# Window attention, softplus layer and four experts on one core: all eighteen attention groups scheduled ahead of the dense layers, a third buffer for k and q chunks

## Chip, cores, metric

One core of one Trainium2 chip. The metric is the device time of one execution in microseconds (us). TensorE (PE) multiplies matrices, VectorE (DVE), ScalarE (ACT) and GpSimd (POOL) do element-wise work, SyncE (SP) issues the transfers. PEld is the loading of PE's weights, which overlaps PE.

## What is computed

```python
# attention, window 64, 2 batches, 8 heads, 576 positions, head size 64
scores = where(mask, q @ k.T / 8, -1e9); attn = softmax(scores); x = attn @ v    # x: 1152 x 512
h = x @ w_in                                                                      # 512 -> 2048
g = maximum(h, 0) + log1p(exp(-abs(h)))                                           # softplus
x1 = g @ w_out                                                                    # 2048 -> 512
p = domain_probs / (domain_probs.sum(-1) + 1e-9)
out = sum over 4 experts e of p[:, e] * (maximum(x1 @ w1[e], 0) @ w2[e])          # 512 -> 1024 -> 512
```

All inputs are float32, except that `w_in` and `w_out` come as 64-bit words, whose upper and lower halves the kernel turns into pairs of float32 itself.

## The kernel before

**Attention.** 18 groups of 64 positions each. A group has three pieces of PE work: scores `s` (L961, from a chunk of k, `kT`, and of q, `qT`, each serving three groups), transposes `p` (L989) and the product with v `o` (L1001). Between them DVE masks and takes the largest score (L968, four per group), ACT takes exponentials (L972, four), DVE inverts the sums (L976, L977), the four halves of `p` are scaled (L984 on ACT, L980 on DVE or POOL), the transposed `pT` is copied out of PSUM (L248), and the result `o` is split into a high part (L248 copy) and a low part (L1013, DVE) of `x`, in three blocks `x0`, `x1`, `x2` of 384 positions.

**The softplus layer**, the first dense stage. Its weights come in 16 chunks: two transfers into a raw buffer `r` (three of them), then `convert`: magnitude (L390, ACT), and on DVE hold (L394), rest (L397), place (L401), sign (L405), power (L408), whole (L411) and low (L414); the high part is copied by ACT or POOL. Then 4 units x 3 blocks x 4 chunks = 48 steps. A step is 12 matmuls `h` (L467), the softplus chain (ACT: L486, L489, L495, L501; DVE: lost L498, with_max L504; a subtraction `l<-l,w` and, after a cast by ACT to `g`, a subtraction `g<-l,g`, both at the helper's line L267), and 12 matmuls into four accumulators `acc` (L537). Sums over units go to `part` (L565).

**The experts**, the second dense stage, take seven products of halves instead of eight (L702, banks x, y, z) and 32 second products (L797); their weights are split into a high copy (L248) and a low subtraction (L267), with sums `S` of weight blocks.

**The order** of every engine's queue is made when the program is built. Each piece is an `Op` with the engines that may do it, and a due time; `plan` walks a model of the engines and always takes the piece that is ready and due first. Its numbers stand in `P`: `T0` is when the first dense step is due, `ATT` the spacing of attention groups before it, `E_...` which engines may do a kind of piece ("V" or "D" DVE, "A" ACT, "G" POOL). Groups 0 to 5 (block 0) are due before `T0`; groups 6 to 17 are due between the dense steps of unit 0. Each engine then runs its queue strictly in that order. A `Ring` says how many buffers a kind of tile has; a piece waits for the last reader of the buffer it takes.

Of the kernel before, what the change touches and what calls it, by code (L numbers as in the profile page):

```python
# [21 lines left out]
def kernel(  # L22
# [51 lines left out]
    AHEAD = 2  # L74
# [71 lines left out]
    class Ring:  # L146
# [10 lines left out]
        def take(self, first):  # L157
# [5 lines left out]
                                         we=EARLY, wl=LATE, p=3, pT=2, kT=2, v=5).items()}  # L163
# [191 lines left out]
    def convert(c, first, last, due):  # L355
# [97 lines left out]
    def step(s, u, blk, f, tag, due1, due2):  # L453
# [33 lines left out]

        def exponential():
# [22 lines left out]
        o1 = Op({"A": (ACT(tb, True), magnitude)}, [o] + re.next())  # L511
# [336 lines left out]
    def load_qk(c, due):  # L848
        b, s = c // CPB, (c % CPB) * CH

        def keys(k0, k1):
            if c not in kT:
                kT[c] = ap_.tile([128, NP, W + CH], F32, tag="kT", bufs=2, name=f"kT{c}")
            nc.sync.dma_start(out=kT[c][:, :, k0:k1], in_=k[b, :, :, s - W + k0:s - W + k1].rearrange("h p s -> p h s"))

# [13 lines left out]
        for k0, k1, g0, g1 in parts:  # L869
            there = [Op({"Q": ((k1 - k0) * 0.0057, lambda k0=k0, k1=k1: keys(k0, k1))}, after, due, 2.2)]  # L870
# [7 lines left out]
    def load_v(c, due):  # L878
        b = c // CPB
        for i in range((c % CPB) * GPC, (c % CPB + 1) * GPC):  # L880
# [11 lines left out]
            v_there[b, i] = Op({"Q": (0.75, fn)}, ring.next(), due, 2.2)  # L892
            v_done[b, i] = ring.take(v_there[b, i])

    class Group:
# [19 lines left out]
        def scores(self, due):  # L915
# [13 lines left out]
            for hp in range(NP):  # L929
# [3 lines left out]
                scaled.append(Op({e: how[e] for e in (P.E_P if self.blk else P.E_P0)}, [o]))  # L933
            self.p_there = scaled

        def transposes(self, due):
# [3 lines left out]
            o = Op(copies(512, self.transposed, True, P.E_T if self.blk else P.E_T0), [o] + pT.next())  # L940
# [3 lines left out]
        def values(self, due):  # L944
# [4 lines left out]
            o1 = Op(copies(KC * W, lambda: self.to_x()[1::-1], True, P.E_H if self.blk else P.E_H0), [o, *first_x[-1:]])  # L949
# [119 lines left out]
    groups = [Group(n, ("att", "h", "acc") if n < GPB[0] else ("att",) * 3) for n in range(NT // W)]  # L1069
    x_due0 = [P.T0 - P.ATT * (GPB[0] - 1 - n) for n in range(6)]  # L1070
# [120 lines left out]
```

## Time and profile before

| what | us |
|---|---|
| median of 3 runs (654.02 to 654.44) | 654.33 |
| the profiled execution, its time | 654.69 |
| its span in the profile | 652.6 |
| time around the span (difference) | 2.1 |
| PE busy / DVE busy / ACT busy / POOL busy | 629.6 / 505.3 / 356.9 / 192.6 |

The profile gives, for one execution, what each engine did and when. A row of instructions has a mean duration; neighbours on one engine overlap by their start-up, so the distance from one start to the next is some tenths of a microsecond shorter than the duration, and sums are made with that distance. Idle time of an engine is what is left of a window when its busy time is taken off.

### The profile page before, as it was taken

How to read it: one execution, taken by the hardware profiler on the slowest of the kernel's cores; microseconds unless marked ns; L12 is line 12 of the kernel's file. 1: busy time of each engine (PE TensorE's matmuls, PEld its weight loads, DVE VectorE, ACT ScalarE, POOL GpSimd, SP SyncE). 2: the span in 40 equal slices, each digit the busy share in tenths (PEclk: the TensorE clock that was granted, in tenths of full speed). 3: DMA queues.
4: the chain of work that ended last, by engine and by line, in shares of the span. 5: the costliest groups of instructions: out<-in, count | busy, mean ns of one | idle time of the engine just before them, and what ended most of it. 6: DMA issues, size and time to landing. Idle time of an engine off the chain costs nothing.

```text
span 652.6 us, 10673 instructions
## 1 busy us (share of the span) xinstructions
PE 629.6 (96%) x4008; PEld 577.7 (89%) x4008; DVE 505.3 (77%) x1002; ACT 356.9 (55%) x778; POOL 192.6 (30%) x166
## 2 busy tenths in 40 slices
PE   7679999999999999999999999999999999999997
PEld 6467889999999999898999989998989998989996
DVE  4999989999999998985756575585796687767643
ACT  6999988867676775643334244323634352535230
POOL 2212452101002641643305132160453342613310
PEclk9999999999999999999999999999999999999999
DMA  8954212222130410013112311231243313131001
GB/s 277 379 177 171 98 65 76 96 76 77 65 131 28 163 68 2 0 65 130 65 64 74 122 64 66 74 122 64 66 154 121 124 71 130 65 129 65 2 1 64
DMA packets 30515, 62.83 MB, mean 96 GB/s; under 512 B 2816, under 2 KB 6016, under 8 KB 30464
## 3 DMA queue, kind: packets, MB, share of 16 engines
q1 hardware_dynamic: 30464, 62.16, 27.0%
q8 instruction: 31, 0.51, 0.3%
q14 instruction: 20, 0.16, 0.1%
HBM read 59.79 MB, written 2.36 MB: 95 GB/s over the span
## 4 chain that ended last, share of the span: by engine, by line
PE 60%; DVE 28%; ACT 6%; issue 3%; DMA 2%; SPq 0%; DVEq 0%; ACTq 0%
PE acc L797 28%; PE y L702 11%; PE z L702 7%; PE x L702 7%; DVE w L498 3%; DVE g L267 3%; DVE l L504 3%; PE acc L537 2%; DVE part L565 2%; DVE kh L405 2%; DVE km L411 2%; DVE l L267 2%; DMA qT<-in_q_dram 2%; DVE w L414 2%; ACT p L972 2%
## 5 line engine op out<-in xcount | busy, mean ns | idle before, releaser
L797 PE MATMUL acc<-wb,G 128*128 128x512 f32 x864 | 213.6, 392 | 0.0
L797 PEld LDWEIGHTS acc<-wb,G 128*128 128x128 f32 x864 | 157.2, 188 | 28.7 <-DVE G L771 0.3
L537 PE MATMUL acc<-g,w 128*128 128x384 f32 x576 | 110.9, 340 | 2.2 <-DVE g L267 1.6
L467 PE MATMUL h<-x,w 128*128 128x384 f32 x576 | 105.9, 335 | 0.2 <-ACT w L248 0.2
L537 PEld LDWEIGHTS acc<-g,w 128*128 128x128 f32 x576 | 99.7, 188 | 5.9 <-DVE g L267 3.1
L267 POOL TENSOR_TENSOR wc<-S,wc 128x1024 fp32r<-128x1024 f32 x19 | 49.3, 2593 | 187.9 <-ACT wc L248 187.9
L467 PEld LDWEIGHTS h<-x,w 128*128 128x128 f32 x576 | 100.3, 188 | 0.9 <-ACT w L248 0.5
L767 ACT ACTIVATE G<-C 128x256 fp32r<-128x256 f32 (+2 forms) x64 | 35.8, 562 | 72.4 <-PE acc L797 50.2
L771 DVE SCALAR_TENSOR_TENSOR G<-C,G 128x256 fp32r<-128x256 f32 (+2 forms) x64 | 43.9, 686 | 30.2 <-ACT G L767 29.7
L248 ACT ACTIVATE wa<-rq 128x512 fp32r<-128x512 f32 x64 | 30.9, 515 | 59.9 <-PE y L702 56.1
L702 PE MATMUL y<-xo,wc 128*128 128x320 f32 (+1 forms) x384 | 62.1, 297 | 0.9 <-DVE q L723 0.8
L702 PE MATMUL z<-xo,wc 128*128 128x320 f32 (+1 forms) x384 | 61.6, 296 | 0.0
L267 POOL TENSOR_TENSOR l<-l,w 128x384 f32<-128x384 f32 x19 | 25.6, 1347 | 121.1 <-DVE l L504 100.7
L702 PE MATMUL x<-xo,wa 128*128 128x320 f32 (+1 forms) x384 | 61.3, 295 | 0.0
L702 PEld LDWEIGHTS x<-xo,wa 128*128 128x128 f32 x384 | 57.1, 189 | 3.4
L702 PEld LDWEIGHTS y<-xo,wc 128*128 128x128 f32 x384 | 55.4, 190 | 3.4 <-DVE q L723 1.6
L248 ACT ACTIVATE wc<-S 128x1024 fp32r<-128x1024 f32 x32 | 33.7, 1053 | 41.3 <-PE z L702 36.7
L702 PEld LDWEIGHTS z<-xo,wc 128*128 128x128 f32 x384 | 54.8, 190 | 0.1
L267 POOL TENSOR_TENSOR wa<-rq,wa 128x512 fp32r<-128x512 f32 (+1 forms) x32 | 38.8, 1220 | 26.4 <-ACT wa L248 22.8
L771 DVE SCALAR_TENSOR_TENSOR G<-x,G 128x320 fp32r<-128x320 f32 (+1 forms) x32 | 14.6, 457 | 34.2 <-ACT G L767 34.2
L767 ACT ACTIVATE G<-x 128x320 fp32r<-128x320 f32 (+1 forms) x32 | 13.1, 411 | 47.4 <-PE x L702 47.4
L267 DVE TENSOR_TENSOR wb<-rq,wb 128x1024 fp32r<-128x1024 f32 x29 | 35.4, 1222 | 2.6 <-ACT wb L248 1.4
(88 smaller groups left out, 984.9 us busy)
## 6 DMA issues: line engine op xcount, KB each, us to landing
rq<-in_moe_w_dram SPq DMA_DIRECT2D x64, 512.0 KB, 4.2
r<-in_moe_w_in_dram SPq DMA_DIRECT2D x16, 512.0 KB, 3.6
r<-in_moe_w_out_dram SPq DMA_DIRECT2D x16, 512.0 KB, 4.7
v<-in_v_dram SPq DMA_DIRECT2D x16, 256.0 KB, 5.2
out_dram<-tot SPq DMA_DIRECT2D x9, 256.0 KB, 2.1
kT<-in_k_dram SPq DMA_DIRECT2D x4, 512.0 KB, 4.6
qT<-in_q_dram SPq DMA_DIRECT2D x5, 384.0 KB, 6.3
kT<-in_k_dram SPq DMA_DIRECT2D x1, 384.0 KB, 6.6
```

The costliest lines, as they stand in the source:

```text
L248: nc.scalar.activation(out, in_, AF.Copy)
L267: engine.tensor_tensor(out, in0, in1, op=op)
L405: nc.vector.scalar_tensor_tensor(h, word(1), 0xc0000000, h, op0=ALU.bitwise_and, op1=ALU.bitwise_or)
L411: nc.vector.scalar_tensor_tensor(f32(env["m"]), word(0), 2.0 ** -32, env["m"], op0=ALU.mult, op1=ALU.add)
L467: nc.tensor.matmul(h, lhsT=a[:, wi, kc, :], rhs=x[:, xi, kc, :], start=n == 0, stop=n == 3 * KC - 1)
L498: nc.vector.scalar_tensor_tensor(env["w"], env["w"], 1.0, env["e"], op0=ALU.subtract, op1=ALU.subtract)
L504: nc.vector.scalar_tensor_tensor(env["l"], env["h"], 0.0, env["l"], op0=ALU.max, op1=ALU.add)
L537: nc.tensor.matmul(acc[:, :BLK[blk]], lhsT=b[:, wi, i * 128:(i + 1) * 128], rhs=g[:, gi, :], start=start, stop=stop)
L702: nc.tensor.matmul(env[bank], lhsT=w[:, a, wi, kc * 128:(kc + 1) * 128], rhs=b[xi][:, kc, :], start=first and m == 0, stop=m == 5, skip_gr ...
L767: nc.scalar.activation(env["g", c][:, HI, a:a + w], of[what](), AF.Relu)
L771: nc.vector.scalar_tensor_tensor(g[:, LO, a:a + w], of[what](), 0.0, f32(g[:, HI, a:a + w]), op0=ALU.max, op1=ALU.subtract)
L797: nc.tensor.matmul(acc, lhsT=g[:, gi, i * 128:(i + 1) * 128], rhs=b[:, wi, :], start=j == 0 and m == 0, stop=j == QPE - 1 and m == 5)
```

## The change

The six groups that used the early rules (own engine choices, PSUM banks of three kinds `att`, `h`, `acc`) become eighteen (`FIRST=18`); all are due before `T0`, 1.54 us apart, and `T0` moves from 32.94 to 41.21. The first `FIRST` groups use `E_T0="AD"` and `E_H0="AD"` (copies of `pT` and of `x` by ACT or DVE; before ACT alone), `E_P0="AG"` (scaling by ACT or POOL; before DVE too). `kT` and `qT` have three buffers. The first four weight chunks may have their magnitude taken by DVE and their hold by POOL (`NABS=4`). In unit 0 the subtraction `l<-l,w` goes to DVE (`E_S0="V"`; before POOL). Casts of `g`, of weights (`E_G`, `E_W1`, `E_W2`) may go to ACT or DVE; the other numbers that set due times are new throughout.

```diff
-        T0=32.94, ATT=1.39, ..., SLACK=-0.89,
-        MERGED=1, FUS=(4, 4, 4, 4), WIDE=0, AHEAD1=2, DW2=33.65, DV=3.24, DQ=13.62, DW=23.71,
-        E_W1="A", E_W2="A", ..., E_G="A", E_F="A", E_X="AV", E_T="A", E_H="AD", E_R="A", E_S="VG", E_L="V", E_P="AG",
-        E_T0="A", E_H0="A", E_P0="AVG", E_W0="AG", E_R0="A", E_G0="A", E_S0="G", E_L0="VG")
+        T0=41.21, ATT=1.54, ..., SLACK=-14.92,
+        MERGED=1, NABS=4, FIRST=18, AHEAD=2, FUS=(4, 4, 4, 4), WIDE=0, AHEAD1=2, DW2=28.4, DV=9.54, DQ=11.16, DW=20.13,
+        E_W1="AV", E_W2="AV", ..., E_G="AV", E_F="A", E_X="A", E_T="AD", E_H="AD", E_R="A", E_S="VG", E_L="V", E_P="A",
+        E_AB="AV", E_HO="VG", E_A="A", E_A0="A", E_T0="AD", E_H0="AD", E_P0="AG", E_W0="AG", E_R0="A", E_G0="A", E_S0="V", E_L0="VG")
...
-                                         we=EARLY, wl=LATE, p=3, pT=2, kT=2, v=5).items()}
+                                         we=EARLY, wl=LATE, p=3, pT=2, kT=3, v=5).items()}
...
+        early = c < P.NABS
+        how = {"A": (ACT(n), magnitude), "V": (one, magnitude_by_dve)}
+        o_abs = Op({e: how[e] for e in (P.E_AB if early else "A")}, before + kh.next())
+        how = {"V": (two, lambda: hold(nc.vector)), "G": (POOL1(n), lambda: hold(nc.gpsimd))}
+        o_hold = Op({e: how[e] for e in (P.E_HO if early else "V")}, [o_abs])
...
-                kT[c] = ap_.tile([128, NP, W + CH], F32, tag="kT", bufs=2, name=f"kT{c}")
+                kT[c] = ap_.tile([128, NP, W + CH], F32, tag="kT", bufs=3, name=f"kT{c}")
-                            [qk_done[c - 2]] if c >= 2 else (), due, 2.2))
+                            [qk_done[c - 3]] if c >= 3 else (), due, 2.8))
...
-    groups = [Group(n, ("att", "h", "acc") if n < GPB[0] else ("att",) * 3) for n in range(NT // W)]
+    groups = [Group(n, ("att", "h", "acc") if n < P.FIRST else ("att",) * 3) for n in range(NT // W)]
-        if g.blk == 0:
-            x_due.append(P.T0 - P.ATT * (GPB[0] - 1 - j))
+        if g.n < P.FIRST:
+            x_due.append(P.T0 - P.ATT * (P.FIRST - 1 - g.n))
```

What this does to the queues, at three places. In the names, the number after the letter of a tile is its group (`s10`, `p17`) or, for `h`, `g`, `l`, `w`, `e`, its unit, block and chunk (`h0_2_1`: unit 0, block 2, chunk 1); the last number is only a running number.

PE where the first dense step stands, before: it is taken between attention groups 6 and 7.

```order
L961 MATMUL s9_505<-kT3_314,qT3_332 64x128 x8
L1001 MATMUL o6_523<-pT6_498,v0_6_425 64x64 x8
L467 MATMUL h0_0_0_540<-x0_0_354,w0_300 128x384 x12
L989 MATMUL p7_568<-ident_82,p7_420 128x128 x4
L1001 MATMUL o7_585<-pT7_581,v0_7_464 64x64 x8
L961 MATMUL s10_598<-kT3_314,qT3_332 64x128 x8
L989 MATMUL p8_621<-ident_82,p8_466 128x128 x4
L467 MATMUL h0_0_1_635<-x0_0_354,w1_417 128x384 x12
```

The same place of PE after:

```order
L1012 MATMUL o15_948<-pT15_919,v1_6_908 64x64 x8
L1000 MATMUL p17_972<-ident_82,p17_897 128x128 x4
L474 MATMUL h0_0_0_977<-x0_0_276,w0_339 128x384 x12
L1012 MATMUL o16_997<-pT16_942,v1_7_946 64x64 x8
L474 MATMUL h0_0_1_1010<-x0_0_276,w1_610 128x384 x12
L1012 MATMUL o17_1035<-pT17_991,v1_8_994 64x64 x8
L474 MATMUL h0_2_1_1064<-x0_2_836,w1_610 128x384 x12
L548 MATMUL acc0_0_0_1085<-g0_0_0_1062,w0_339 128x384 x3
L548 MATMUL acc0_0_1_1090<-g0_0_0_1062,w0_339 128x384 x3
```

The first dense step now stands behind the transposes of the last group; only two products with v are left behind it, and the third dense step reads block 2, which the last of them completes.

POOL over the first dense steps, before: it scales `p`, and does the subtractions `l<-l,w` of unit 0.

```order
L267 TENSOR_TENSOR l0_0_0_628<-l0_0_0_628,w0_0_0_626 128x384
L267 TENSOR_TENSOR g0_0_0_706<-l0_0_0_628,g0_0_0_706 128x384
L980 TENSOR_SCALAR p10_615<-p10_615,m10_616 128x128 x2
L267 TENSOR_TENSOR l0_0_1_759<-l0_0_1_759,w0_0_1_755 128x384
L980 TENSOR_SCALAR p11_694<-p11_694,m11_695 128x128
L267 TENSOR_TENSOR l0_0_2_852<-l0_0_2_852,w0_0_2_832 128x384
```

The same place of POOL after:

```order
L991 TENSOR_SCALAR p13_713<-p13_713,m13_714 128x128 x3
L398 TENSOR_SCALAR kh2_0_782<-kh2_0_782 128x1024
L991 TENSOR_SCALAR p14_762<-p14_762,m14_763 128x128
L991 TENSOR_SCALAR p15_807<-p15_807,m15_808 128x128 x2
L991 TENSOR_SCALAR p16_855<-p16_855,m16_856 128x128 x3
L256 TENSOR_SCALAR w2_781<-kh2_0_782 128x2x512
L267 TENSOR_TENSOR g0_2_3_1575<-l0_2_3_1532,g0_2_3_1575 128x384
```

One subtraction is left on POOL in the whole of unit 0.

DVE where the first softplus chain ends, after:

```order
L1024 TENSOR_TENSOR x0_2_836<-o16_997,x0_2_836 128x4x64
L514 SCALAR_TENSOR_TENSOR l0_0_0_1030<-h0_0_0_977,l0_0_0_1030 128x384
L508 SCALAR_TENSOR_TENSOR w0_0_0_1026<-w0_0_0_1026,e0_0_0_1007 128x384
L412 TENSOR_SCALAR ke2_0_1047<-kh2_0_782 128x1024
L267 TENSOR_TENSOR l0_0_0_1030<-l0_0_0_1030,w0_0_0_1026 128x384
L1024 TENSOR_TENSOR x0_2_836<-o17_1035,x0_2_836 128x4x64
L418 SCALAR_TENSOR_TENSOR w2_781<-km2_0_963,ke2_0_1047 128x2x512
L267 TENSOR_TENSOR g0_0_0_1062<-l0_0_0_1030,g0_0_0_1062 128x384
```

The low parts of the last two groups stand in one queue with the first softplus chain and the conversion of chunk 2; before, the first chain stood between the masks of groups 10 and 11.

## Rows read from the trace of the kernel before

**Rows 1.** Windows: busy us of each engine per stretch (instructions), granted clock, DMA.

```profile
0.00:34.00 34.00, 23.36 (x301) 19.26 (x302) 22.95 (x123) 25.79 (x99) 8.58 (x25) 0.95 0.90 322
34.00:60.00 26.00, 20.91 (x196) 17.45 (x196) 25.40 (x68) 24.77 (x73) 5.01 (x6) 0.93 0.52 175
60.00:90.00 30.00, 28.99 (x253) 25.40 (x252) 28.66 (x79) 28.52 (x96) 13.15 (x12) 1.00 0.28 95
90.00:240.00 150.00, 149.88 (x900) 148.08 (x899) 146.17 (x236) 111.50 (x221) 34.59 (x25) 1.00 0.25 90
240.00:271.00 31.00, 29.42 (x170) 28.28 (x169) 28.25 (x49) 20.43 (x44) 10.56 (x8) 1.00 0.00 1
271.00:652.60 381.60, 377.03 (x2196) 339.22 (x2195) 253.84 (x454) 145.94 (x253) 120.75 (x92) 1.00 0.23 81
```

**Rows 2.** Timeline of PE: start, length in us, line, tiles, count, idle before.

```profile
4.14 1.97 PE L961 MATMUL s<-kT,qT 64*64 64x128 f32 x16 [4.14 <-DMA qT<-in_q_dram]
13.28 0.69 PE L1001 MATMUL o<-pT,v 128*64 128x64 f32 x16
18.71 1.09 PE L961 MATMUL s<-kT,qT 64*64 64x128 f32 x16 [2.52 <-DMA qT<-in_q_dram]
33.79 2.50 PE L467 MATMUL h<-x,w 128*128 128x384 f32 x12
101.72 10.56 PE L467 MATMUL h<-x,w 128*128 128x384 f32 x60
112.12 2.63 PE L537 MATMUL acc<-g,w 128*128 128x384 f32 x12
268.69 4.49 PE L537 MATMUL acc<-g,w 128*128 128x384 f32 x23 [1.01 <-DVE g L267]
```

**Rows 3.** Groups of DVE by line, 0 to 271 us: count, busy us, mean ns.

```profile
L498 DVE SCALAR_TENSOR_TENSOR w<-w,e 128x384 f32<-128x384 f32 x48 | 30.3, 635 | 0.8 <-ACT w L495 0.8
L267 DVE TENSOR_TENSOR g<-l,g 128x384 fp32r<-128x384 f32 x45 | 28.7, 641 | 3.3 <-ACT g L248 3.1
L565 DVE TENSOR_TENSOR part<-acc,part 128x384 f32<-128x384 f32 x32 | 16.9, 548 | 0.3 <-PE acc L537 0.3
```

**Rows 4.** Groups of POOL by line, 0 to 271 us, the subtraction `l<-l,w`.

```profile
L267 POOL TENSOR_TENSOR l<-l,w 128x384 f32<-128x384 f32 x19 | 25.6, 1347 | 121.1 <-DVE l L504 100.7 <-DVE m L976 10.1 <-DVE w L498 6.5
```

**Rows 5.** Timeline of DVE and POOL around two subtractions on POOL.

```profile
33.18 0.69 DVE L401 TENSOR_SCALAR kh<-kh 128x1024 uint32<-128x1024 uint32 x1
53.50 1.53 DVE L401 TENSOR_SCALAR kh<-kh 128x1024 uint32<-128x1024 uint32 x1
170.94 1.01 DVE L565 TENSOR_TENSOR part<-acc,part 128x384 f32<-128x384 f32 x2
171.87 0.79 DVE L397 TENSOR_SCALAR km<-kh 128x1024 uint32<-128x1024 uint32 x1
...
53.45 1.02 POOL L267 TENSOR_TENSOR l<-l,w 128x384 f32<-128x384 f32 x1 [1.58 <-DVE w L498]
171.09 1.02 POOL L267 TENSOR_TENSOR l<-l,w 128x384 f32<-128x384 f32 x1 [11.12 <-DVE l L504]
```

**Rows 6.** Timeline of ACT in the attention: start, length in us.

```profile
7.00 0.39 ACT L972 ACTIVATE p<-p,m 128x128 f32<-128x128 f32 x1
7.39 0.39 ACT L972 ACTIVATE p<-p,m 128x128 f32<-128x128 f32 x1
11.49 0.68 ACT L984 ACTIVATE p<-p,m 128x128 f32<-128x128 f32 x2
12.07 0.57 ACT L248 ACTIVATE pT<-p 128x512 f32<-128x512 f32 x1
12.55 0.39 ACT L972 ACTIVATE p<-p,m 128x128 f32<-128x128 f32 x1
24.14 0.37 ACT L248 ACTIVATE x<-o 128x256 fp32r<-128x256 f32 x1
24.41 1.14 ACT L390 ACTIVATE kh<-r 128x1024 f32<-128x1024 f32 x1
```

More of the change, by code (lines that the diff above doesn't have):

```diff
@@ L73 @@
     RAW, GB = 3, 3
-    AHEAD = 2
+    AHEAD = P.AHEAD
     PE = lambda n: n / 2400 + 0.0133
@@ L293, in load @@
         free = rings["raw"].next()
-        a = Op({"Q": (1.5, lambda: fn(0))}, free, due, 2.2)
-        b = Op({"Q": (1.5, lambda: fn(1))}, free + [a], due + 1.5, 2.2)
+        a = Op({"Q": (1.5, lambda: fn(0))}, free, due, 2.8)
+        b = Op({"Q": (1.5, lambda: fn(1))}, free + [a], due + 1.5, 2.8)
         raw_there[c] = (a, b), rings["raw"].take(a)
@@ L390, in magnitude, with magnitude_by_dve, hold @@
             nc.scalar.activation(f32(tile_("h", U32, 2)), f32(word(1)), AF.Abs)
-        def hold():
+        def magnitude_by_dve():
+            start()
+            nc.vector.tensor_scalar(tile_("h", U32, 2), word(1), 0x7fffffff, None, op0=ALU.bitwise_and)
+        def hold(engine):
             h = f32(env["h"])
-            nc.vector.tensor_scalar(h, h, TINY, HUGE, op0=ALU.max, op1=ALU.min)
+            engine.tensor_scalar(h, h, TINY, HUGE, op0=ALU.max, op1=ALU.min)
         def rest():
@@ L510, in step @@
         re, rl, rw = (rings[k] for k in "elw")
-        o1 = Op({"A": (ACT(tb, True), magnitude)}, [o] + re.next())
+        how = {"A": (ACT(tb, True), magnitude), "D": (DVE(tb), magnitude_by_dve)}
+        o1 = Op({e: how[e] for e in (P.E_A if u else P.E_A0)}, [o] + re.next())
         e_done = re.take(o1)
@@ L869, in load_qk @@
         for k0, k1, g0, g1 in parts:
-            there = [Op({"Q": ((k1 - k0) * 0.0057, lambda k0=k0, k1=k1: keys(k0, k1))}, after, due, 2.2)]
+            there = [Op({"Q": ((k1 - k0) * 0.0057, lambda k0=k0, k1=k1: keys(k0, k1))}, after, due, 2.8)]
             if g0 == 0:
@@ L891, in load_v @@
             ring = rings["v"]
-            v_there[b, i] = Op({"Q": (0.75, fn)}, ring.next(), due, 2.2)
+            v_there[b, i] = Op({"Q": (0.75, fn)}, ring.next(), due, 2.8)
             v_done[b, i] = ring.take(v_there[b, i])
@@ L932, in scores @@
                        "A": (0.293, lambda hp=hp: self.scaled_by_act(hp))}
-                scaled.append(Op({e: how[e] for e in (P.E_P if self.blk else P.E_P0)}, [o]))
+                scaled.append(Op({e: how[e] for e in (P.E_P if self.n >= P.FIRST else P.E_P0)}, [o]))
             self.p_there = scaled
@@ L939, in transposes @@
             pT = rings["pT"]
-            o = Op(copies(512, self.transposed, True, P.E_T if self.blk else P.E_T0), [o] + pT.next())
+            o = Op(copies(512, self.transposed, True, P.E_T if self.n >= P.FIRST else P.E_T0), [o] + pT.next())
             t_done.append(o)
@@ L1068 @@
     constant = Op({"G": (2.7, masks)}, due=-9.0)
-    groups = [Group(n, ("att", "h", "acc") if n < GPB[0] else ("att",) * 3) for n in range(NT // W)]
-    x_due0 = [P.T0 - P.ATT * (GPB[0] - 1 - n) for n in range(6)]
+    groups = [Group(n, ("att", "h", "acc") if n < P.FIRST else ("att",) * 3) for n in range(NT // W)]
+    x_due0 = [P.T0 - P.ATT * (P.FIRST - 1 - n) for n in range(6)]
     for n in range(2):
```

14 lines of the change are left out of this document (7 added, 7 removed).

## The prediction

> **What bounds the kernel now.** I read the windows first [rows 1]. From 271 us on PE is busy 377.0 of 381.6 us: the experts are bound by PE, and their length is fixed. From 90 to 240 us PE is busy 149.9 of 150. What could be won lies ahead: PE idles 10.6 us up to 34, 5.1 up to 60, 1.0 up to 90, and 1.6 from 240 to 271. But DVE stands beside it. Its idle time is 11.0 us up to 34 (6.3 of it before the first scores are there [rows 2]), then 0.6, 1.3, 3.8 and 2.8: 19.6 us in all, and 251.4 us of work by 271, which is about when it hands over the last `g` of the softplus layer. PE's last wait there is on that DVE subtraction, 1.01 us [rows 2]. So two resources are nearly full up to 271 us: PE, which loses time early, and DVE, which loses almost none after 34. The change helps PE only; what it does to DVE decides.
>
> The view that sizes DVE's hidden loss is its groups [rows 3]: an instruction of 384 columns takes 548 ns where it reads PSUM (L565), but 635 and 641 ns on average at L498 and in `g<-l,g`, which read SBUF alone. Those 87 and 93 ns, times 48 and 45, are 8.4 us. The cause stands in rows 5: L401 takes 0.69 us alone and 1.53 beside a POOL subtraction that runs 1.02, while two L565 beside another such subtraction keep their distance of 0.465 each (170.94 to 171.87). By these rows POOL's two-input work holds up those DVE instructions that need SBUF twice, by up to 0.84 us, and the PSUM readers not at all. I take 0.45 us per POOL subtraction, about half way between 0 and 0.84.
>
> The Trainium skill says this more sharply: in "SBUF — State Buffer", section "Who interferes with whom", DVE and GpSimd share one pair of ports as an exclusive lock, and the second to issue fully blocks for the whole instruction. The 0.84 us of rows 5 agree with a block, the 0.45 with its being avoided about every second time. What the rule would do if it always struck is the first rival below.
>
> **PE's side.** The first dense step is at 33.79 us [rows 2]; after the change it stands behind all transposes. What must pass before it on ACT: 72 exponentials at 0.39 us (7.00 to 7.39), 28.1; 38 scalings at 0.29 (11.49 to 12.07, two), 11.0; nine copies of `pT` at 0.48 (12.07 to 12.55), 4.3; six copies of `x` and three conversion pieces, at most the 0.57 us of a `pT` copy and the 1.14 of L390 each and about 4.6 in all [rows 6]. That is 48.0 us. The first `v` transfer now goes ahead of k and q, so I start ACT at 7.2 instead of about 6.6 (its second exponential is at 7.00 [rows 6]). ACT's idle time between 34 and 60 was 1.2 us, and before 34 it was 8.2 [rows 1], most of it ahead of the first scores; I allow 4 us after the start, since DVE and ACT wait for each other in turn. 7.2 + 48.0 + 4 + 0.6 for the last transposes: the first dense step at **60 us**, 26 later than now.
>
> From there to the matmuls that wait for the last `g`, PE has 48 steps of `h` and 47 of `acc`, 2.08 us each (60 matmuls in 10.40 us, 101.72 to 112.12 [rows 2]), 197.6; four products of the experts taken early, 3.5; and two products with v, 0.69 each: 202.3 us in all. PE alone could be there at 262.3. Now the same point is reached at 269 [rows 2], so PE's side would give 6.4 us, less what it waits.
>
> **DVE's side, up to the same point**, counted in the two queues. Added: 14 `l<-l,w` from POOL at 0.465, 6.5 us [rows 5]; eight copies of `pT`, 512 columns from PSUM, not shown on DVE before: between 0.47 (the 384-column PSUM reader) and 0.69 (L401, 1024 columns); I take 0.6 by columns, 4.8; nine casts of `x`, 256 columns, between 0.27 (the 384-column one by columns, less) and 0.47, taken 0.34: 3.1; two `g<-l,g` and four casts of `g`, 2.0. Taken away: eight scalings (0.2 each, bounded by 0.47), 1.6; three holds, against one magnitude added, 1.3; conversions for the experts that now come later or on POOL, 1.8. Sum **+11.7 us** (9 to 14 by the bounds).
>
> Given back: POOL's two-input subtractions of the softplus layer (19 of `l<-l,w` [rows 4] and three of `g<-l,g`) fall from 22 to 6, 16 x 0.45 = **-7.2 us** (0 to -13.4 by rows 5). POOL takes more of the experts' weights before 254 us, 14 such instructions instead of 10, and three holds of 1024 columns, which rows 5 price at up to 0.84 each: +2. Balance +6.5: 251.4 becomes 257.9 us of work.
>
> DVE's idle time: 6.9 us until the first scores. In the attention 3, as before (4.8 up to 34). Then a turn that did not exist: with_max of the first step waits for `h` at 60 + 2.1 and three ACT pieces, about 64, and the queue holds it behind the low part of group 16 and ahead of that of group 17; DVE has done some 51 us of work by then, which with the waits so far is 61, so 3 us more. Afterwards it idled 7.9 us from 60 to 271 now; with more to do I take 2.5. Sum 15.4. The last `g` is handed over at 257.9 + 15.4 = **273.3 us**, against 271 now: DVE is later than PE (262.3), it sets the end, and the loss is **+2.3 us**.
>
> **What costs nothing.** From the handover on, PE's queue is the same but for a few neighbours that change places, so the experts keep their 381.6 us. Some 23 weight casts move there from ACT to DVE and 18 small sums and five subtractions from DVE to POOL; DVE idles 127.8 and POOL 260.8 of 381.6 us there [rows 1], which hides them. Without that cover a POOL subtraction of 1024 columns in front of a DVE step that PE waits for costs up to a microsecond each; PE's idle time there is 4.6 us now, most of it at the very end. The third buffer for k and q frees SP's queue of a wait: PE stood 2.52 us for `qT` at 18.71 [rows 2]. ACT was busy through that stretch, and it sets the pace of the attention, so I count nothing. What is queued behind the remaining waits in SP's queue: the loads of chunk 4 wait for the conversion of chunk 1, and the last `v` stands behind them; that `v` is needed at about 65 us and should land a microsecond or two ahead.
>
> **Sum.** Profile 654.69 + 2.3 = 657.0; the median of the runs is 0.36 below the profiled execution: **656.6 us**.
>
> **Rivals.**
> 1. *Faster: POOL's retreat gives back more.* If each of the 16 subtractions had cost DVE its full 1.02 us, DVE gets 16.3 instead of 7.2 us, and its last `g` is due at 264.2. Then PE sets the end: 262.3 plus the 2.7 us that it idles after 60 now [rows 1] and 1 at the turn, 266, against 271: -5, about **650 us**. Rows 3 speak against it (the mean stretch is 90 ns); for it, that my idle times for DVE are guesses of the same size. It decides as soon as DVE's work falls below about 253 us by the handover. This is the skill's lock rule ("SBUF — State Buffer") striking every time; the trace shows it partly.
> 2. *The same.* DVE loses no further idle time in the turn and afterwards less than 1 us: 273.3 - 2.3 = 271, **654.3 us**. DVE's mere 3.8 us of idle time in 150 [rows 1] speaks for it.
> 3. *Slower by more: the attention itself takes longer.* Three engines hand over within each group, and dense work no longer fills the gaps. At 64 instead of 60 us DVE's end moves along: **660.5 us**. The 10.6 us of PE waits before 34 speak for it, the third buffer against.
> 4. *The change does not do what it says.* It does, by the queues; but if PE's granted clock falls to its lower level in the sparse attention (0.95 and 0.93 are the means up to 60 us [rows 1], with stretches at the low one) and dense steps begin there, PE loses a few microseconds early, which DVE's lateness covers. No time of its own.
>
> **How the numbers follow.** The forecast (DVE bound, +1.3 to +5) has 0.38, rival 3 with everything beyond 0.08, rival 2 0.21, rival 1 0.33. A measurement of this kernel can tell about 0.2%, 1.3 us, from no change. So slower 0.46, same 0.21, faster 0.33. The likeliest case alone reaches from 655.6 to 659.5; the range must take in rival 1 down to 650 and rival 3 up to 661, and leaves out about 2 in 10.
>
> **What would show it.** In the profile after: the first dense `h` at 58 to 62 us; few subtractions on POOL between 60 and 200, and a mean of L498 near 570 ns; DVE idle about 6 us between its first instruction and 65, and under 4 from there to the last `g`; that `g` at 272 to 275, with PE waiting for it by more than the 1.01 us of now; PE busy from there as before. I am wrong if PE is at its last `acc` of the softplus layer before 268 us: then DVE had less work than counted or was blocked less. I am wrong the other way if PE waits inside the experts.

## The result, and the profile after

The changed kernel takes 658.46 us (median of 8 runs, 655.86 to 659.76) against 654.37 for the kernel before, run beside it (8 runs). The ratio is 1.0061, with a 95% interval of 1.0042 to 1.0079: slower by 4.1 us. The profiled execution took 659.76 us, the slowest of the eight, with a span of 658.0.

The stretches of [rows 1], as the windows of the changed kernel show them (length, busy us of PE, PEld, DVE, ACT and POOL with their instructions, granted clock, share of DMA, GB/s):

```profile
0.00:34.00 34.00, 25.46 (x356) 21.01 (x356) 22.54 (x128) 25.92 (x109) 14.47 (x32) 1.00 0.93 319
34.00:60.00 26.00, 19.05 (x255) 14.84 (x256) 22.89 (x105) 23.09 (x88) 13.72 (x19) 0.85 0.28 103
60.00:90.00 30.00, 28.43 (x175) 26.14 (x172) 28.31 (x45) 19.94 (x38) 1.42 (x1) 0.90 0.41 149
90.00:240.00 150.00, 148.82 (x856) 147.95 (x855) 149.06 (x244) 111.14 (x219) 23.41 (x18) 1.00 0.25 85
240.00:271.00 31.00, 28.99 (x159) 28.35 (x158) 27.47 (x50) 19.27 (x40) 9.06 (x7) 0.94 0.11 35
```

Two differences from [rows 1] matter below. POOL works 28.2 us up to 60 us instead of 13.6, and the granted clock is 0.85 and 0.90 in the two windows around the first dense step and 0.94 in the last window, where it was 0.93, 1.00 and 1.00 before. From 90 to 240 both PE and DVE are busy over 148 of 150 us; before, DVE was busy 146.2.

PE's timeline shows the turn from attention to dense work (start, length, line, tiles, count, idle before):

```profile
40.40 0.79 PE L1000 MATMUL p<-ident,p 128*128 128x128 f32 x4 [2.21 <-POOL p L991]
53.43 0.66 PE L1000 MATMUL p<-ident,p 128*128 128x128 f32 x4 [0.84 <-POOL p L991]
55.08 0.79 PE L1000 MATMUL p<-ident,p 128*128 128x128 f32 x4 [0.99 <-POOL p L991]
58.04 1.25 PE L1000 MATMUL p<-ident,p 128*128 128x128 f32 x4 [1.15 <-POOL p L991]
61.87 4.19 PE L474 MATMUL h<-x,w 128*128 128x384 f32 x12
```

The transposes wait 5.2 us for scalings of `p` on POOL, the first dense step begins at 61.87 us (33.79 before [rows 2]), and its twelve matmuls take 4.19 us; twelve took 2.50 in the kernel before.

POOL's groups up to 66 us say why the scalings are late (count, busy us, mean ns, idle before):

```profile
L991 POOL TENSOR_SCALAR p<-p,m 128x128 f32<-128x128 f32 x34 | 13.7, 419 | 25.4 <-DVE m L979 13.3 <-ACT p L983 5.8 <-DVE m L988 3.9
L398 POOL TENSOR_SCALAR kh<-kh 128x1024 f32<-128x1024 f32 x3 | 10.9, 3624 | 2.1 <-DVE kh L394 1.1 <-ACT kh L390 1.1
```

Each hold (L398) occupies POOL for 3.62 us, and the scalings stand behind it in POOL's queue.

DVE's groups up to 300 us, the rows that answer to [rows 3]:

```profile
L267 DVE TENSOR_TENSOR g<-l,g 128x384 fp32r<-128x384 f32 x47 | 29.8, 634 | 1.9 <-ACT g L248 1.8
L508 DVE SCALAR_TENSOR_TENSOR w<-w,e 128x384 f32<-128x384 f32 x48 | 28.4, 594 | 1.3 <-ACT w L505 1.2
L267 DVE TENSOR_TENSOR l<-l,w 128x384 f32<-128x384 f32 x43 | 26.9, 625 | 0.2
L576 DVE TENSOR_TENSOR part<-acc,part 128x384 f32<-128x384 f32 x36 | 18.9, 547 | 0.7 <-PE acc L548 0.7
```

L508 (L498 before) falls from 635 to 594 ns. The last `g` is handed over at 275.0 us (270.9 before), and from there to the end of the span pass 383.0 us (381.7 before). So the loss of this execution, 5.4 us of span, lies ahead of that handover with 4.1 and in the experts with 1.3.

### The profile page after: what moved, and what is told of

It is laid out like the page before. It is cut to its first block, busy times and chain, and to the rows that moved or that the text cites. A ratio compares the mean times of both kernels' runs of the same rounds, so it can differ in the third digit from the quotient of the medians.

```text
span 658.0 us, 10683 instructions
## 1 busy us (share of the span) xinstructions
PE 631.8 (96%) x4008; PEld 581.1 (88%) x4008; DVE 522.5 (79%) x1041; ACT 327.5 (50%) x727; POOL 198.2 (30%) x178
## 3 DMA queue, kind: packets, MB, share of 16 engines
HBM read 59.79 MB, written 2.36 MB: 94 GB/s over the span
## 4 chain that ended last, share of the span: by engine, by line
PE 81%; DVE 13%; ACT 3%; issue 2%; POOL 1%; DMA 1%; SPq 0%; ACTq 0%
PE acc L808 28%; PE h L474 12%; PE acc L548 12%; PE y L713 11%; PE z L713 7%; PE x L713 7%; PE s L972 1%; DVE p L979 1%; DVE g L267 1%; DVE G L782 1%; DVE w L508 1%; DVE w L418 1%; DVE pT L252 1%; DVE x L1024 1%; DVE xo L267 1%
## 5 line engine op out<-in xcount | busy, mean ns | idle before, releaser
L548 PE MATMUL acc<-g,w 128*128 128x384 f32 x576 | 107.8, 337 | 3.6 <-DVE part L576 2.0
L474 PE MATMUL h<-x,w 128*128 128x384 f32 x576 | 109.4, 341 | 0.8 <-ACT x L248 0.8
L474 PEld LDWEIGHTS h<-x,w 128*128 128x128 f32 x576 | 103.1, 193 | 1.7 <-ACT x L248 0.9
L778 ACT ACTIVATE G<-C 128x320 fp32r<-128x320 f32 (+3 forms) x64 | 36.0, 562 | 85.8 <-PE acc L808 57.9
L782 DVE SCALAR_TENSOR_TENSOR G<-C,G 128x320 fp32r<-128x320 f32 (+3 forms) x64 | 44.2, 692 | 12.9 <-ACT G L778 12.6
L267 POOL TENSOR_TENSOR wa<-rq,wa 128x512 fp32r<-128x512 f32 (+1 forms) x28 | 34.5, 1239 | 16.4 <-ACT wa L248 16.4
L493 ACT ACTIVATE e<-h 128x384 f32<-128x384 f32 x48 | 23.4, 487 | 21.1 <-PE h L474 17.8
L983 ACT ACTIVATE p<-p,m 128x128 f32<-128x128 f32 x72 | 27.9, 390 | 8.2 <-DVE m L979 6.2
L713 PEld LDWEIGHTS y<-xo,wa 128*128 128x128 f32 x192 | 28.7, 189 | 3.4 <-DVE r L734 1.1
L511 ACT ACTIVATE l<-e 128x384 f32<-128x384 f32 x48 | 24.9, 518 | 13.6 <-DVE g L267 13.4
```

The costliest lines, as they stand in the source:

```text
L267: engine.tensor_tensor(out, in0, in1, op=op)
L474: nc.tensor.matmul(h, lhsT=a[:, wi, kc, :], rhs=x[:, xi, kc, :], start=n == 0, stop=n == 3 * KC - 1)
L493: nc.scalar.activation(tile_("e"), env["h"], AF.Abs)
L511: nc.scalar.activation(tile_("l"), env["e"], AF.Ln, bias=1.0)
L548: nc.tensor.matmul(acc[:, :BLK[blk]], lhsT=b[:, wi, i * 128:(i + 1) * 128], rhs=g[:, gi, :], start=start, stop=stop)
L713: nc.tensor.matmul(env[bank], lhsT=w[:, a, wi, kc * 128:(kc + 1) * 128], rhs=b[xi][:, kc, :], start=first and m == 0, stop=m == 5, skip_gr ...
```

## The experiments

**Theories.** (a) As the prediction had it: DVE's added work makes the last `g` late. (b) The holds on POOL hold up the scalings of `p`, and so the end of the attention. (c) The granted clock falls in the sparse attention, and the first dense step pays for it. To be weighed with them: the third buffer, the early attention as such, and the waits in the experts.

Unless said otherwise an experiment keeps the order of instructions of the changed kernel and alters only who carries a step out. The table gathers the profiled executions: the start of the first dense matmul, the handover of the last `g`, the stretch between, and the rest of the span; beside it the ratio of the times to the kernel before, measured beside it, with its 95% interval. What an experiment costs or returns against the changed kernel is the difference of their ratios, times 654.37 us, unless medians are named.

| kernel | first `h` | last `g` | stretch | rest | ratio |
|---|---|---|---|---|---|
| before | 33.79 | 270.9 | 237.1 | 381.7 | 1 |
| changed | 61.87 | 275.0 | 213.1 | 383.0 | 1.0061 [1.0042, 1.0079] |
| e1 holds on DVE | 58.54 | 270.6 | 212.1 | 383.0 | 1.0024 [1.0007, 1.0041] |
| e2 copies on ACT | 64.75 | 276.9 | 212.1 | 383.0 | 1.0124 [1.0097, 1.015] |
| e3 `l - w` on POOL | 63.48 | 280.3 | 216.8 | 383.0 | 1.0157 [1.013, 1.0184] |
| e4 filler from the 7th group | 64.57 | 275.8 | 211.2 | 383.0 | 1.011 [1.0084, 1.0136] |
| e5 two buffers | 75.13 | 287.5 | 212.3 | 383.0 | 1.0279 [1.0251, 1.0308] |
| e6 early attention alone | 61.77 | 281.1 | 219.3 | 381.2 | 1.0158 [1.0132, 1.0185] |
| e7 e1 + filler in 5 groups | 59.60 | 270.8 | 211.2 | 383.0 | 1.0002 [0.9986, 1.0017] |
| e8 e1 without the lost part | 58.30 | 266.6 | 208.3 | 383.0 | 0.9961 [0.9944, 0.9978] |
| e9 e7 + first `v` later | 58.25 | 269.4 | 211.1 | 383.1 | 1.0012 [0.9994, 1.0031] |
| e10 e9 + casts of `g` on ACT | 59.12 | 268.6 | 209.5 | 383.1 | 1.0003 [0.9985, 1.0021] |
| e11 e10 + experts' casts on ACT | 59.31 | 272.6 | 213.2 | 389.5 | 1.0106 [1.0084, 1.0129] |

**e1: the holds back on DVE.**

```diff
-        how = {"V": (two, lambda: hold(nc.vector)), "G": (POOL1(n), lambda: hold(nc.gpsimd))}
+        how = {"V": (two, lambda: hold(nc.vector)), "G": (POOL1(n), lambda: hold(nc.vector))}
```

> The changed kernel with its three holds issued by VectorE instead of POOL, every other instruction in the same place. If the holds on POOL are what makes the first dense step late (three of 3.62 us each, with the scalings of p behind them and TensorE waiting 2.21 + 0.84 + 0.99 + 1.15 = 5.2 us for those): first dense matmul near 59 us instead of 61.87 and about 655.5 us in all (3 under the changed kernel's 658.5). If VectorE's work is what sets the end: three holds of about 0.7 us more on it, 658.5 to 660. If the clock alone costs the 4 us: the first dense step earlier, but still at half clock, 657 to 658.5.

Measured: 655.31 us, ratio 1.0024 against 1.0061, so 2.4 of the 4.1 us come back; the two intervals do not overlap. The first dense matmul moves from 61.87 to 58.54, and the last `g` follows. On DVE a hold takes 0.68 us. Theory (b) holds; more work on DVE made the kernel faster, which (a) does not allow. What remains is in three rows of PE's timeline and three of the 2-us windows:

```profile
51.70 0.96 PE L1000 MATMUL p<-ident,p 128*128 128x128 f32 x4 [1.43 <-POOL p L991]
54.66 1.25 PE L1000 MATMUL p<-ident,p 128*128 128x128 f32 x4 [1.38 <-POOL p L991]
58.54 3.86 PE L474 MATMUL h<-x,w 128*128 128x384 f32 x12
```

```profile
54.00:56.00 2.00, 1.32 (x7) 0.82 (x8) 2.00 (x8) 2.00 (x7) 1.07 (x3) 0.76 0.00 0
56.00:58.00 2.00, 1.69 (x18) 1.13 (x18) 1.97 (x6) 1.97 (x8) 0.00 (x0) 0.50 0.24 37
60.00:62.00 2.00, 2.00 (x8) 2.00 (x7) 2.00 (x2) 0.00 (x0) 0.00 (x0) 0.53 0.64 260
```

PE still idles 1.43 and 1.38 us, the clock falls to its lower level (0.50, 1.2 GHz), and the first dense step takes 3.86 us.

**e4 and e7: matmuls that only keep PE busy.** Both put this ahead of the transposes of a group; e4 from the seventh group on, in the changed kernel, e7 in the last five groups of e1.

```diff
             self.t = self.bank(1, [128, NP, 128])
+            for n in range(4 if self.n >= FROM else 0):
+                nc.tensor.matmul(self.t[:, n % NP, :], lhsT=ident, rhs=ident, start=True, stop=True)
```

> The changed kernel with four matmuls of ident by ident ahead of the transposes of each group from the seventh on; what they write, the transposes write over, so the output is the same. They add 48 matmuls, about 0.85 us for each group at full clock, into the stretch in which TensorE waits for p and its granted clock is at half. If the half clock of 56 to 66 us costs the first dense step about 2 us and more behind it: first dense step 2.3 us long instead of 4.19 and 655 to 657 us. If TensorE's own work in the attention sets its end: 10 us of work more, first dense matmul at 65 us or later, 660 to 665. If neither: 658.5.

> The holds on VectorE as in the run e1_hold_dve, and four matmuls of ident by ident ahead of the transposes of the last five groups only (written over by the transposes), where e1 showed TensorE waiting 1.43 and 1.38 us at 51.7 and 54.7 and then half the clock from 55 to 62. If the half clock costs the first dense step its 2 us: that step 2.3 us long, and about 2 us under e1, 653 to 654. If the filler only delays the transposes: 655 to 657.

Measured: e4 660.63 us, 1.011; e7 654.12, 1.0002. Each group's four calls are eight instructions in the trace and take about 1.0 us (0.85 was expected). The clock stayed at its upper level in both: in e7 all four 2-us windows from 54 to 62 show 1.00. The window from 34 to 65 us, in the changed kernel and then in e4, and e4's first dense step:

```profile
34.00:65.00 31.00, 23.71 (x271) 18.81 (x271) 27.89 (x111) 26.18 (x95) 13.72 (x19) 0.80 0.36 129
34.00:65.00 31.00, 28.77 (x373) 24.41 (x368) 26.64 (x117) 26.44 (x98) 14.77 (x19) 1.00 0.29 95
```

```profile
64.57 2.35 PE L475 MATMUL h<-x,w 128*128 128x384 f32 x12
```

The clock stays at 1.00, where the changed kernel had 0.80 from 34 to 65, and the first step takes 2.35 us instead of 4.19. But PE is now busy 28.77 of 31 us, and the first dense matmul comes 2.7 us later, more than the shorter stretch (211.2 against 213.1) returns. In e7 most of the filler falls into PE's waits:

```profile
59.60 2.36 PE L475 MATMUL h<-x,w 128*128 128x384 f32 x12
```

The first dense step takes 2.36 us instead of 3.86, starts 1.1 us later than in e1, and the median falls by 1.2 us. The intervals of e1 and e7 overlap a little (1.0007 to 1.0041 and 0.9986 to 1.0017), so the size is uncertain; the shorter step and the shorter stretch are plain in the profile. Theory (c) holds, with one to two us: 1.5 and 1.8 by the first dense step alone (e7 against e1, e4 against the changed kernel). With the holds and the clock mended the changed kernel ties with the kernel before.

**e2: the copies of `pT` and `x` back on ACT.**

```diff
-        how = {"A": (ACT(n, psum), by_act), "D": (DVE(n), by_dve), ...
+        how = {"A": (ACT(n, psum), by_act), "D": (DVE(n), by_act if swap else by_dve), ...
...
-    ... P.E_T if self.n >= P.FIRST else P.E_T0)
+    ... P.E_T if self.n >= P.FIRST else P.E_T0, True)
```

> The changed kernel with the 8 copies of pT and the 9 of x that the attention of the changed kernel gives VectorE (5.4 + 4.2 = 9.6 us of it) issued by ScalarE instead, same places. If VectorE's added work sets the end, as the prediction had it: 4 us or more come back, about 654. If ScalarE or the chain from p to x sets the end of the attention: nothing or a loss, 658 to 661, the first dense matmul at 62 to 64 us.

Measured: 661.46 us, 1.0124: 4.1 us slower than the changed kernel, though DVE lost 9.6 us of work. In the window from 34 us to the first dense matmul ACT is nearly full and DVE is not:

```profile
34.00:64.70 30.70, 22.64 (x280) 16.98 (x281) 21.34 (x103) 29.41 (x111) 13.81 (x20) 0.83 0.27 87
```

So in e2 ACT sets the end of the attention, and everything after starts later by as much: the stretch from the first dense matmul is 212.1 us as in e1. Theory (a) falls for this part: the copies on DVE are a gain.

**e3: `l - w` of unit 0 back on POOL.**

```diff
-        how = {"V": (DVE(n), lambda: by(nc.vector)), "G": ...
+        how = {"V": (DVE(n), lambda: by(nc.gpsimd if swap else nc.vector)), "G": ...
...
-... P.E_S if u else P.E_S0), [o5, o6])
+... P.E_S if u else P.E_S0, not u), [o5, o6])
```

> The changed kernel with the twelve subtractions l - w of unit 0 issued by POOL, as before the change, same places; it takes 7.5 us from VectorE and gives POOL some 12 of about 1 us. If VectorE's work between 60 and 275 us sets the end: 2 to 5 us faster, 654 to 656.5. If TensorE sets it from about 80 us on, as the chain of waits of the changed kernel says: no change, 657.5 to 659.5.

Measured: 663.59 us, 1.0157, 6.3 us slower than the changed kernel; of this 3.7 us lie in the stretch from the first dense matmul (216.8 against 213.1), where the moved steps are. The first dense matmul itself came 1.6 us later in the profiled execution, ahead of every moved step; that part is not explained. Two pairs of the timelines of POOL and DVE show the price:

```profile
75.26 1.39 POOL L267 TENSOR_TENSOR l<-l,w 128x384 f32<-128x384 f32 x1 [3.23 <-DVE l L514]
82.69 1.40 POOL L267 TENSOR_TENSOR l<-l,w 128x384 f32<-128x384 f32 x1 [6.04 <-DVE l L514]
...
75.82 1.92 DVE L409 SCALAR_TENSOR_TENSOR kh<-r,kh 128x1024 uint32<-128x1024 uint32 x1
83.25 1.39 DVE L405 TENSOR_SCALAR kh<-kh 128x1024 uint32<-128x1024 uint32 x1
86.17 1.21 DVE L409 SCALAR_TENSOR_TENSOR kh<-r,kh 128x1024 uint32<-128x1024 uint32 x1
88.24 0.68 DVE L412 TENSOR_SCALAR ke<-kh 128x1024 uint32<-128x1024 uint32 x1
```

L409 takes 1.92 us beside a subtraction on POOL and 1.21 without; L405 takes 1.39 where L412, of the same shape, takes 0.68; L412 starts ahead of the next subtraction, which begins at 88.39 us. So a subtraction on POOL costs DVE 0.71 us in both pairs, more than it saves by not running on DVE (0.47 start to start), and the POOL instruction itself takes 1.39 us, where the two of [rows 5] took 1.02. The whole stretch says the same:

```profile
63.50:280.30 216.80, 209.63 (x1199) 204.91 (x1198) 211.02 (x328) 151.16 (x297) 55.54 (x40) 0.98 0.23 83
```

With twelve instructions fewer DVE is busy 211.0 us, against 207.0 in the changed kernel. The twelve were 5.6 us (0.47 each) to 7.5 (their mean of 0.625), so as an estimate each one on POOL cost DVE 0.8 to 1.0 us. PE then waits for `g` at 79.39, 93.14 and 116.01 us, 0.77 to 0.91 us each.

**e8: DVE relieved where it is full.** e1 with the lost part left out, 48 instructions and 28 us of DVE by their durations; the subtraction then takes a wrong term, so this shows a price and is no version to use.

```diff
         def lost():
-            nc.vector.scalar_tensor_tensor(env["w"], env["w"], 1.0, env["e"], op0=ALU.subtract, op1=ALU.subtract)
+            pass
```

> e1_hold_dve without the 48 instructions that form the lost part (w - 1 - e), which the subtraction from l then doesn't get: 28 us less of VectorE between the first dense matmul and the last g, and wrong low digits. The stretch from the first dense matmul to the last g was 212.1 us in e1; TensorE's own work in it is 206.9. If VectorE sets the stretch: it falls to TensorE's 207 or 208, and the time by 4 to 5 us, to 650 or 651. If TensorE sets it and its waits there come from the chain within a step: 211 or more, 654 to 655.

Measured: 651.51 us, 0.9961, 3.8 us under e1 by the medians, and the stretch is 208.3 us. Over that stretch, e1 and then e8:

```profile
58.50:270.60 212.10, 206.79 (x1199) 203.62 (x1198) 208.15 (x340) 151.24 (x297) 36.91 (x28) 0.99 0.25 85
```

```profile
58.30:266.60 208.30, 205.99 (x1199) 203.47 (x1198) 188.05 (x292) 150.63 (x297) 34.97 (x28) 0.99 0.25 87
```

DVE goes from 208.15 to 188.05 us busy, and the stretch comes down to 2.3 us above PE's 206; PE's waits for DVE in it fall from 4.5 to 1.5 us. So in the changed order DVE and PE are both full after the attention (208.15 and 206.79 of 212.10 us in e1), and taking 20 us of busy time from DVE returns only 3.8. In the runs that keep this order (e3, e8 and e11 apart) the stretch varies from 209.5 to 213.1 us and the first dense matmul from 58.25 to 75.13: what moves the end is above all when the stretch begins.

**e5: two buffers for the chunks of k and q.**

```diff
-tag="kT", bufs=3 ... tag="qT", bufs=3
+tag="kT", bufs=2 ... tag="qT", bufs=2
```

> The changed kernel with two buffers instead of three for the chunks of k and of q; all instructions stay in the changed kernel's places. If the third buffer is worth nothing, as the prediction had it: no change, 657 to 659, first scores and first dense matmul as in the changed kernel (5.78, 61.87). If it carries the early attention (the loads of the next chunk wait for the scores of the chunk two before): TensorE waits for k or q between 15 and 50 us and the first dense matmul comes 2 us or more later, 660 or above.

Measured: 672.27 us, 1.0279, 14.3 us more than the changed kernel; the first dense matmul comes at 75.13 us. PE's timeline, and SP's queue around it (SP issues nothing between its first and second row here):

```profile
46.26 1.12 PE L1012 MATMUL o<-pT,v 128*64 128x64 f32 x16 [5.03 <-DMA v<-in_v_dram]
49.56 1.12 PE L1012 MATMUL o<-pT,v 128*64 128x64 f32 x16 [1.13 <-DMA v<-in_v_dram]
...
32.73 0.46 SPq L291 DMA_DIRECT2D r<-in_moe_w_out_dram  x1
41.27 0.38 SPq L865 DMA_DIRECT2D kT<-in_k_dram  x1
41.69 0.50 SPq L899 DMA_DIRECT2D v<-in_v_dram  x1
```

The load of k waits 8.0 us for the scores that free its buffer, the load of v stands behind it in SP's queue, and PE then waits 5.03 us for that v. The loads of q wait for scores too, 19.0 us in three waits. In this order the third buffer is worth 14 us; the waits for v are 6.2 of them, and the rest is not split up. It is not needed for an early attention as such: e6 has two buffers, with an order made for two, and begins its dense work at 61.77.

**e6: the early attention alone.** The kernel before, with these edits; the early rules of engines then hold for all eighteen groups (copies of `pT` and `x` by ACT, scaling by ACT, DVE or POOL), and the order is made anew by the planner.

```diff
-        T0=32.94, ATT=1.39, ...
+        T0=41.21, ATT=1.54, FIRST=18, ...
...
-    groups = [Group(n, ("att", "h", "acc") if n < GPB[0] else ("att",) * 3) ...
+    groups = [Group(n, ("att", "h", "acc") if n < P.FIRST else ("att",) * 3) ...
```

> The kernel before with the attention moved alone: all eighteen groups due ahead of the dense layers, in the changed kernel's kinds of PSUM banks and with its two due times for x, but with the old two buffers, the old engines for every step (holds on VectorE, copies of pT and x on ScalarE, l - w of unit 0 on POOL) and the old due times elsewhere. If the choice of engines is what costs (holds on POOL, copies and l - w on VectorE): about 653 to 655, at or under the kernel before. If the early attention itself costs, since ScalarE and VectorE bound it at about 3.1 us a group and TensorE idles meanwhile: 660 or above, first dense matmul at 60 to 66 us, and the stretch from it to the last g about 212 to 217 us.

Measured: 664.17 us, 1.0158, 10.3 us slower than the kernel before. The stretch from the first dense matmul is 219.3 us, and PE's timeline shows its start:

```profile
67.36 0.62 PE L467 MATMUL h<-x,w 128*128 128x384 f32 x2 [0.91 <-ACT w L248]
69.22 5.86 PE L467 MATMUL h<-x,w 128*128 128x384 f32 x24 [1.25 <-DVE w L414]
75.58 2.03 PE L467 MATMUL h<-x,w 128*128 128x384 f32 x10 [0.51 <-DVE w L414]
80.13 2.21 PE L537 MATMUL acc<-g,w 128*128 128x384 f32 x11 [2.34 <-DVE g L267]
83.93 1.34 PE L467 MATMUL h<-x,w 128*128 128x384 f32 x6 [0.96 <-DVE w L414]
```

PE waits 6.0 us between 62 and 90 for converted weights and `g`, with DVE busy 27.8 of these 28 us. The early attention is the losing part of the change: the new engines, the third buffer and the due times together return 6 of its 10 us. How much of the 10 is due to the old due times, which were not fitted to an early attention, was not tried.

**e9, e10 and e11: what is left.** e9 issues the first load of v behind the first k and q; e10 also gives ACT the four casts of `g` that the plan gives DVE; e11 also gives ACT twenty casts of the experts' weights.

```diff
+        order = plan()
+        order.remove(v_there[0, 0])
+        order.insert(order.index(qk_there[0][-1][1]) + 1, v_there[0, 0])
...
-        ... "V": (DV2(n), by_dve), ...
+        ... "V": (DV2(n), by_act if swap else by_dve), ...
...
-        o8 = Op(copies(tb, high, engines=P.E_G if u else P.E_G0), ...
+        o8 = Op(copies(tb, high, engines=P.E_G if u else P.E_G0, swap=True), ...
...
-            o1 = Op(copies(..., engines=P.E_W2), ...
+            o1 = Op(copies(..., engines=P.E_W2, swap=True), ...
```

> e7_hold_filler with the first load of v issued behind the first chunk's k and its first two loads of q, where the changed kernel issues it ahead of all (the kernel before began its scores at 4.14 us, the changed one at 5.78, e7 at 6.47). If the start moves the whole attention, VectorE and TensorE being busy from there on: about 1 us faster than e7, 653. If the weights' loads or the copies set the pace up to 34 us: no change, 654.

> e9_v_later with the four casts of g that the plan gives VectorE in the dense layers (0.35 us each) issued by ScalarE (0.52 us), same places. If VectorE still sets a part of TensorE's waits there: up to 1.4 us faster than e9. If the longer chain of the step costs as much: within 0.5 us of e9.

> e10_g_act with the 20 casts of the experts' weights (wb, wc) that the plan gives VectorE issued by ScalarE, same places. In the changed kernel TensorE waits 2.0 us for q in the experts (0.8 in the kernel before). If these casts, standing ahead of q on VectorE, cause that: about 1.2 us faster than e10, 653.3, and the stretch from the last g to the end 381.8 us instead of 383.0. If the order around q causes it: no change, 654.5.

Measured: e9 655.28 us, 1.0012; e10 654.54, 1.0003; e11 661.50, 1.0106. In e9 the scores start at 4.16 us instead of 6.47, and the profiled span is 1.3 us shorter than that of e7, but the medians do not show it: no gain can be told. Nor for e10. In e11 the waits for q are gone (2.0 us in the changed kernel and in e10), and the experts take 6.4 us more: PE now waits six times for `G`, 3.8 us in all, and is itself busy 4.6 us longer, which is not explained (chain of waits of e11):

```profile
303.89 0.74 ACT G L779
304.63 0.96 ACT wb L249
305.61 0.68 DVE wb L268
306.75 3.04 DVE G L783
309.84 0.51 PE acc L809
```

The cast on ACT ends late, DVE's subtraction for the same weights waits for it, and the step `G` behind that in DVE's queue is what PE needs. No version that computes the whole result beat the kernel before by more than can be measured; e7, e9 and e10 equal it.

## Why the prediction was right, and where its steps were not

It forecast +2.3 us, with +1.3 to +5 for its likeliest case; +4.1 was measured. Sign and size were right, and the last `g` came at 275.0 (forecast 273.3, expected between 272 and 275). The mechanism is only partly the one it gave. Of its signs, PE's wait for the last `g` of more than 1.01 us failed: PE works on two products of 12 matmuls from 272.60 us, and no wait is shown (PE's timeline, then DVE's row of that `g`):

```profile
272.60 4.63 PE L548 MATMUL acc<-g,w 128*128 128x384 f32 x24
277.07 1.39 PE L713 MATMUL y<-xo,wc 128*128 128x320 f32 x6
274.15 0.85 DVE L267 TENSOR_TENSOR g<-l,g 128x384 fp32r<-128x384 f32 x1
```

From 272.60 to 277.07 is 4.47 us, and 24 matmuls at the prediction's 2.08 us per 12 need 4.16; so PE can have waited 0.3 us there at most. The mean of L508 is 594 ns, not near 570, and DVE idled 6.2 us from 65 us to the last `g`, not under 4. The two windows that end at the first dense matmul and at the last `g`:

```profile
0.00:61.87 61.87, 46.04 (x616) 36.69 (x617) 47.30 (x234) 50.74 (x202) 28.19 (x51) 0.92 0.64 222
61.87:275.00 213.13, 208.70 (x1199) 205.28 (x1198) 206.96 (x340) 151.20 (x297) 37.89 (x28) 0.98 0.24 85
```

So DVE worked 254.3 us by the handover where 257.9 were forecast, and idled 20.7 where 15.4 were: the date of the last `g` came near because the two misses nearly cancelled, which was luck.

**First dense step at 60 us:** it came at 61.87. The missing term is the holds. They were priced as three holds of "up to 0.84 each" that cost DVE a little; they took 3.62 us each on POOL, and the cost went to the scalings of `p` in the same queue, which that step did not look at. e1 gives their price: 3.3 us of the first dense step, 2.4 us of the time. With the holds on DVE that step begins at 58.54, so the sum on ACT was if anything too long. DVE's idle time ahead of the first dense matmul was 14.6 us where 9.9 (6.9 and 3) were counted; with the holds on DVE it was 11.1.

**PE alone at 262.3:** the stretch was counted as 202.3 us of work without a wait (its terms add up to 202.5). In the changed kernel PE's last dense products start about 213 us after the first dense matmul: 4.4 us of waits, and 2.1 us more for the first step alone because it ran at half clock. The remaining 4 us are not split up; a second fall of the clock to 0.50, at 248 to 250 us, is a part of them. So PE is not 11 us ahead of DVE but abreast of it. DVE does hold PE up: 3.6 of the 4.4 us of waits are for it (2.0 for `part`, 1.6 for `g`), and relieving it is worth 3.8 us (e8). How much of that is new against the kernel before no run separates.

**Rival 4, the clock:** the fall was foreseen, and put down as covered by DVE's lateness, with no time of its own. Since the end moves with the attention's end and PE is abreast, it is not covered: e7 against e1 shows about one us. The single executions agree: within one kernel the time goes with the mean granted clock, in the changed kernel from 655.86 us at 0.994 to 659.76 at 0.986, in the kernel before (72 runs beside the experiments) from 651.6 to 653.8 at 0.997 and above to 656.0 to 657.3 at 0.990 and below. The changed kernel's mean over its eight runs is 0.990, the other's 0.994; at the changed kernel's slope of about 0.5 us per 0.001 some 1.5 to 2 of the 4.1 us go with the lower clock, an estimate.

**DVE's added work, +11.7:** with all its terms the count of DVE's work was 3.6 us too high; the larger fault was to treat the added work as the loss, which fails for its largest parts. The copies of `pT` and `x`, 7.9 us in the sum, free ACT, which sets the attention: undone, they cost 4.1 us (e2). The subtractions `l - w`, 6.5 us against 7.2 given back, so nearly nothing on balance: undone, they cost 3.7 us in the stretch where they stand and 6.3 in all (e3). The 0.45 us taken for one on POOL was too small; e3's pairs show 0.71, its stretch 0.8 to 1.0. By the Trainium skill, "SBUF — State Buffer", section "Who interferes with whom", the shared ports of DVE and GpSimd are an exclusive lock, and against DVE in a two-port mode whoever issues first has them for the whole instruction while the other fully blocks; e3's 0.71 us are nearer to that than the halfway value.

**The early attention itself** has no term of its own in the sum. It is the loss: +10.3 us with the old engines and an order of its own (e6), of which the other edits give back 6. The forecast came out near because what it counted too dear (copies, subtractions) and what it left out (holds, clock, attention) nearly cancelled; to that extent its size was luck.

**Third buffer worth nothing:** wrong in this order, by 14 us (e5). The reasoning looked at one wait for `qT` that ACT's work covered; it did not ask what two buffers would do in the new order, where loads of v stand behind the load of k in SP's queue.

**Experts unchanged at 381.6:** 383.0 or 383.1, in the changed kernel and in all experiments that keep its order there but e11. PE waits 2.0 us for q (0.8 before), which is nearly the whole difference and which the prediction named as a sign of being wrong. The early attention alone does not bring it: in e6, with the old engines and due times in the experts, the rest is 381.2 and the wait for q 0.6. Whether the casts moved to DVE delay q stays open: in e11 they are on ACT and the waits for q are gone, but four of PE's waits for `G` lie ahead of the first of them and all six ahead of the second, so q had more time.

**Rivals 1, 2 and 3:** POOL's retreat gave DVE back more than the 0.45 us each that were taken, if e3's 0.71 to 1.0 hold for all; but as PE is abreast and starts its dense work late, it could not become a gain. Rival 3, an attention that takes longer and moves the end along with it, had a chance of 0.08, and it is what the table of first dense matmuls shows: 61.87 instead of 60, and the measured 658.46 us stand about half way between the forecast's 656.6 and that rival's 660.5.

## What to carry to other kernels

Where a stage is moved ahead of the work that used to fill its gaps, find the engine that sets the stage's own end and price the start of what follows: here 3.3 us of a later first dense step became 2.4 us of time, while 20 us of busy time taken from a full engine behind it returned 3.8. A step given to an idle engine is not free if shorter steps that the critical engine needs stand behind it in that engine's queue. And a buffer count is judged by everything queued behind the load that waits for the buffer.

## What the runs showed of the hardware

- The hold (a maximum and a minimum against two constants, 128x1024, fp32) took 3.62 us on POOL in the changed kernel and 0.68 on DVE in e1, while on POOL the cast of the same size at L256 (a multiplication and an addition of constants) took 1.05 at 29.16 us. The Trainium skill, "GPSIMD Engine Reference", section "4.1 Engine selection", calls one-input elementwise work there roughly line-rate; the hold does not agree. Why it takes so long was not looked into.
- Forty-eight calls that multiply `ident` by `ident` (96 instructions in the trace) kept the granted clock at 1.00 from 34 to 65 us, where it had been 0.80, and the first dense step fell from 4.19 to 2.35 us; but the median rose from 658.46 to 660.63 us (e4). Twenty, placed mostly where PE waits, brought the median from 655.31 to 654.12 us (e7 against e1).
- In the changed kernel the granted clock fell to its lower level (0.50, 1.2 GHz) at about 56 us without a long idle time ahead of it: PE was busy 1.01 of 2 us in the window before, and its waits from 42 to 56 us were of 0.99 us at most. It stayed there through the first dense step and was back at 0.98 in the window from 66 us:

```profile
54.00:56.00 2.00, 1.01 (x9) 0.61 (x10) 1.97 (x11) 2.00 (x11) 0.72 (x2) 0.96 0.00 0
56.00:58.00 2.00, 0.90 (x16) 0.71 (x14) 1.97 (x9) 1.93 (x6) 0.39 (x2) 0.50 0.04 8
64.00:66.00 2.00, 2.00 (x9) 1.56 (x7) 2.00 (x3) 0.00 (x0) 0.35 (x1) 0.50 0.36 147
66.00:68.00 2.00, 2.00 (x25) 1.93 (x25) 0.59 (x2) 1.87 (x5) 1.08 (x1) 0.98 0.60 205
```
